# Attention, layer norm and a SiLU feed-forward in one kernel: head triples across chunks, a progressive layer norm, block transposes, one chain for both last projections

## Chip, cores, metric

One core of one Trainium2 chip. The metric is the device time of one execution in microseconds (us). A run more than 1.5% above the fastest of its kernel counts as slow and is left out. A ratio is the mean time of one kernel's fast runs over the mean of the other kernel's fast runs of the same rounds, so it is not quite the ratio of the medians that are quoted beside it.

## The reference

```python
# x: (1, 2048, 640) bf16; H = 32 heads of Dh = 20; one shared K and V head; F = 1728
xn = (x - mean(x)) / sqrt(var(x) + 1e-5)
q  = (xn @ wq).reshape(1, S, 32, 20).transpose(0, 2, 1, 3)
k, v = xn @ wk, xn @ wv                       # (1, 2048, 20) each
p  = softmax(einsum("bhqd,bkd->bhqk", q, k) * 20 ** -0.5)
o  = einsum("bhqk,bkd->bhqd", p, v)
out = x + o.transpose(0, 2, 1, 3).reshape(1, S, 640) @ wo + silu(xn @ w1) @ w2
```

There are 32 x 2048 x 2048 exponentials, and all of them go through ScalarE.

## The kernel before

Queries are handled in 4 chunks of 512 columns. Within a chunk the heads go in groups of three (the last group has two). For each group the 16 key tiles are walked: one *step* is up to three score matmuls (K = 32, side by side in different rows of the array), one exponential over their PSUM banks (128x1536), and up to three value matmuls (side by side in different columns) that add into U. Everything else on TensorE (queries of the next chunk, FFN, output projection) is *side work*. It goes through one PSUM bank, in pieces between the steps, in program order.

```python
for qc in range(QC):                      # 4 chunks
    for g in range(NG):                   # 11 groups: 10 of three heads, 1 of two
        for kt in range(KT):              # 16 key tiles
            steps.append((qc, g, kt))     # 704 steps
# ... (cut)
for t in range(T):
    # ... (cut)
    if t + NSB < T:
        emit_S(t + NSB, 1)                # scores, two steps ahead
    emit_PV(t)
    # ... (cut)
    if kt == KT - 1:
        schedule_U_pipeline(t, misc)      # copy U, 4 f32 TensorE transposes, normalise
    misc_step(BUDGET)                     # BUDGET = 1.1: two 512-wide side matmuls

def misc_step(budget):
    spent = 0.0
    while spent < budget:
        # ... (cut: take the next job)
        job = cur_job[0]
        last = job_emit_mm(job)           # the last matmul also queues VectorE's eviction
        spent += job.weight
        if last:
            cur_job[0] = None             # ... and the next job starts in the same step
```

Before the loop come the layer norm of all 16 row tiles (square root on ScalarE), their TensorE transposes, all of K and V and the first chunk's queries. After it come the transposes of the last chunk's output and its projection.

The softmax here doesn't subtract the row's maximum and nothing guards it: scores larger than these inputs give would overflow.

Of the kernel before, what the change touches and what calls it, by code (L numbers as in the profile page):

```python
# [7 lines left out]
BF16 = mybir.dt.bfloat16  # L8
# [4 lines left out]
P = 128  # L13
D = 640
H = 32
DH = 20
DC = 5
HSLOT = 32
GH = 3
HT = 8  # L20
NE = 4
NHS = 4
BANK = 512
XB = 7
UB = 6
QW = 512
QTP = QW // P
NSB = 2
HWID = 512
HPH = HWID // QW  # L30


class _Prog:

    def __init__(self):
        self.lists = {k: [] for k in ("pe", "act", "dve", "pool", "sp")}
        self.last_wait = {k: {} for k in self.lists}
        self.cnt = defaultdict(int)

    def emit(self, eng, fn):  # L40
        self.lists[eng].append(fn)

    def wait(self, eng, sem, val):
        if val <= 0:
            return
        key = id(sem)
        if self.last_wait[eng].get(key, 0) >= val:
            return
        self.last_wait[eng][key] = val
        self.lists[eng].append(lambda e, s=sem, v=val: e.wait_ge(s, v))  # L50

    def inc(self, sem):
        self.cnt[id(sem)] += 1
        return self.cnt[id(sem)]

    def emit_inc(self, eng, fn, sem):
        val = self.inc(sem)
        self.lists[eng].append(lambda e, fn=fn, s=sem: fn(e).then_inc(s, 1))
        return val


class _Job:
    def __init__(self, name, bank, mms, consumer, cons_eng, cons_sem, pre_waits=(),
                 weight=1.0, after=None, cons_waits=()):
        self.name = name
        self.bank = bank
        self.mms = list(mms)
        self.consumer = consumer
        self.cons_eng = cons_eng
        self.cons_sem = cons_sem  # L70
        self.pre_waits = list(pre_waits)
        self.cons_waits = list(cons_waits)
        self.weight = weight
        self.after = after
        self.idx = 0
        self.min_iter = -1
        self.use_no = None
        self.ready_val = None
        self.cons_val = None


def build(nc, A_x, A_wq, A_wk, A_wv, A_wo, B_x, B_w1, B_w2, out, stack):
    S = A_x.shape[1]
    F = B_w1.shape[1]
    assert A_x.shape[2] == D and S % HWID == 0
    NT = S // P
    QC = S // QW
    KT = S // P
    NHB = S // HWID
    FC = (F + P - 1) // P  # L90
    FLAST = F - (FC - 1) * P
    NG = (H + GH - 1) // GH
    groups = [list(range(g * GH, min(H, (g + 1) * GH))) for g in range(NG)]
    attn_scale = 1.0 / math.sqrt(DH)
    EPS = 1e-5

    pr = _Prog()
    W = pr.wait
    E_ = pr.emit
    EI = pr.emit_inc  # L100

    def sem(name):
        return stack.enter_context(nc.semaphore(name))

    sb_count = [0]

    def sb(shape, dt):
        sb_count[0] += 1
        return stack.enter_context(nc.sbuf_tensor(f"sbt{sb_count[0]}", shape, dt))

    ps = stack.enter_context(nc.psum_tensor("psall", [P, 8 * BANK], F32))

    def bk(b, lo=0, hi=BANK, rows=P):
        return ps[0:rows, b * BANK + lo: b * BANK + hi]

# [3 lines left out]
    XR = 6  # L119
    x_ring = sb([P, XR, D], BF16)  # L120
    xres = sb([P, QTP, D], BF16)
    xn_ring = sb([P, 4, D], BF16)
    xnT = sb([P, DC, S], BF16)
    stats6 = sb([P, NT, 2, 6], F32)
    mv = sb([P, NT, 2], F32)
    rstd = sb([P, NT], F32)
    stdv = sb([P, NT], F32)
    nbias = sb([P, NT], F32)
    ident_b = sb([P, P], BF16)
    ident_f = sb([P, P], F32)  # L130

    wq_st = sb([P, DC, D], BF16)
    wq_pad = sb([P, DC, HT * P], BF16)
    wk_rep = sb([P, DC, P], BF16)
    wv_aug = sb([P, DC, HSLOT], BF16)
    wo_sb = sb([P, DC, D], BF16)
    w1_sb = sb([P, DC, F], BF16)
    w2_sb = sb([P, FC, D], BF16)

    kT_rep = sb([P, S], BF16)  # L140
    v_aug = sb([P, KT, HSLOT], BF16)
    qT = sb([P, HT, 2, QW], BF16)

    Ebuf = sb([P, NE, GH * QW], BF16)
    U_sb = sb([P, 2, QW], F32)
    rL = sb([P, QTP, GH], F32)
    o_norm = sb([P, 2, QTP, D], BF16)
    oT = sb([P, 2, DC, QW], BF16)
    h_half = sb([P, NHS, HWID], BF16)
    t_buf = sb([P, NHS, HWID], BF16)  # L150
    hT = sb([P, 2, FC, HWID], BF16)
    yx = sb([P, QTP, D], F32)
    out_stage = sb([P, 3, D], BF16)

    s_xload = [sem(f"xload{i}") for i in range(XR)]
    s_xres = [sem(f"xres{i}") for i in range(QTP)]
    s_outdma = [sem(f"outdma{i}") for i in range(3)]
    s_wsmall = sem("wsmall")
    s_w1 = sem("w1")
    s_w2 = sem("w2")  # L160
    s_wo = sem("wo")
    s_stats = sem("stats")
    s_std = sem("std")
    s_nb = sem("nb")
    s_xn_a = sem("xna")
    s_xn_d = sem("xnd")
    s_xnT_d = sem("xnTd")
    s_xnT_a = sem("xnTa")
    s_ident = sem("ident")
    s_pmem = sem("pmem")  # L170
    s_prepq = sem("prepq")
    s_wkv = sem("wkv")
    s_prepkv = sem("prepkv")
    s_kT = sem("kT")
    s_v = sem("v")
    s_q = sem("q")
    s_S = sem("S")
    s_E = sem("E")
    s_PV = sem("PV")
    s_Ufree = sem("Ufree")  # L180
    s_norm = sem("norm")
    s_hh = sem("hh")
    s_th = sem("th")
    s_hc = sem("hc")
    s_y = sem("y")
    s_oT = sem("oT")
    s_outp = sem("outp")
    s_ldve = sem("ldve")
    s_lpool = sem("lpool")
    bank_ready = [sem(f"bkr{b}") for b in range(8)]  # L190
    bank_uses = [0] * 8
    bank_last_free = [None] * 8

    def job_start(job):
        b = job.bank
        job.use_no = bank_uses[b]
        bank_uses[b] += 1
        for (s_, v_) in job.pre_waits:
            W("pe", s_, v_)
        if bank_last_free[b] is not None:  # L200
            W("pe", bank_last_free[b][0], bank_last_free[b][1])

    def job_emit_mm(job):
        k = job.idx
        last = (k == len(job.mms) - 1)
        f = job.mms[k]
        b = job.bank
        if last:
            job.ready_val = EI("pe", lambda pe, f=f, b=b: f(pe, b), bank_ready[b])
        else:  # L210
            E_("pe", lambda pe, f=f, b=b: f(pe, b))
        job.idx += 1
        if last:
            ce = job.cons_eng
            for (s_, v_) in job.cons_waits:
                W(ce, s_, v_)
            W(ce, bank_ready[b], job.ready_val)
            run = job.consumer(b)
            job.cons_val = EI(ce, lambda e, run=run: run(e), job.cons_sem)
            bank_last_free[b] = (job.cons_sem, job.cons_val)  # L220
            if job.after is not None:
                job.after(job)
        return last

    def run_job_now(job):
        job_start(job)
        while not job_emit_mm(job):
            pass

    xv = A_x[0].rearrange("(n p) d -> p n d", p=P)  # L230
    outv = out[0].rearrange("(n p) d -> p n d", p=P)
    xn_val = {}

    def sp_load_x_tile(n):
        slot = n % XR
        if n >= XR:
            for (s_, v_) in xn_val[n - XR]:
                W("sp", s_, v_)
        pr.inc(s_xload[slot])
        E_("sp", lambda e, n=n, slot=slot: e.dma_start(x_ring[:, slot, :], xv[:, n, :]).then_inc(s_xload[slot], 16))  # L240

    stats_val = {}

    std_val = {}
    nb_val = {}

    def dve_ln_stats(n):
        slot = n % XR
        half = D // 2
        W("dve", s_xload[slot], 16 * (n // XR + 1))  # L250
        EI("dve", lambda v, n=n, slot=slot: v.bn_stats(stats6[:, n, 0, :], x_ring[:, slot, 0:half]), s_ldve)
        c2 = EI("dve", lambda v, n=n, slot=slot: v.bn_stats(stats6[:, n, 1, :], x_ring[:, slot, half:D]), s_ldve)
        W("dve", s_ldve, c2)
        c3 = EI("dve", lambda v, n=n: v.bn_aggr(mv[:, n, :], stats6[:, n, :, :]), s_ldve)
        W("dve", s_ldve, c3)
        stats_val[n] = EI("dve", lambda v, n=n: v.tensor_scalar_add(stdv[:, n:n + 1], mv[:, n, 1:2], EPS), s_stats)

    def act_ln_sqrt(n):
        W("act", s_stats, stats_val[n])
        std_val[n] = EI("act", lambda a, n=n: a.activation(stdv[:, n:n + 1], stdv[:, n:n + 1], AF.Sqrt), s_std)  # L260

    def dve_ln_rstd(n):
        W("dve", s_std, std_val[n])
        c4 = EI("dve", lambda v, n=n: v.reciprocal(rstd[:, n:n + 1], stdv[:, n:n + 1]), s_ldve)
        W("dve", s_ldve, c4)
        nb_val[n] = EI("dve", lambda v, n=n: v.scalar_tensor_tensor(
            out=nbias[:, n:n + 1], in0=mv[:, n, 0:1], scalar=-1.0, in1=rstd[:, n:n + 1],
# [748 lines left out]
```

## Time and profile before

The median of the first three runs was 1109.26 us (1108.57 to 1115.64).

| stage of the trace | us |
|---|---|
| start to first exponential | 56.6 |
| first group of 16 steps | 23.5 |
| the other 43 groups, to the end of the last exponential | 1014.2 |
| tail | 15.3 |

The page of the kernel before, its busy table and three rows of its 40 slices. A digit is the busy share of a slice in tenths, 9 meaning 90% or more; the clock row is the granted TensorE clock (the share of full speed that its throttle lets it run at) in tenths.

```profile
span 1109.5 us, 13550 instructions
...
PE 917.3 (83%) x5519; PEld 255.4 (23%) x5580; DVE 220.5 (20%) x600; ACT 1000.1 (90%) x819; POOL 24.3 (2%) x61
...
PE   3778789888888878888898878888898878888888
...
ACT  5599999999989998999989998999998988989994
...
PEclk9899979765579998988559997989557988886556
```

ScalarE (ACT) is the busiest, yet never full for long. The clock row shows that TensorE (PE) ran many stretches at half speed.

Groups of instructions of the kernel before: line, engine, operation, shapes, count, then busy us, mean ns of one, and the idle time just before them with what ended it. L663 is the exponential, L688 the TensorE transpose of U.

```profile
L663 ACT ACTIVATE sbt<-psall 128x1536 bf16<-128x1536 f32 (+1 forms) x704 | 947.1, 1453 | 70.0 <-PE psall L590 65.1
...
L688 PE MATMUL psall<-sbt 96*128 96x96 f32 (+1 forms) x176 | 39.8, 318 | 33.1 <-DVE sbt L681 13.4
```

The exponentials wait 65.1 us for score matmuls (L590). The timeline of ScalarE (start us, length us, what, how many) gives the price of one exponential:

```profile
332.56 6.82 ACT L663 ACTIVATE sbt<-psall 128x1536 bf16<-128x1536 f32 x5 [0.28 <-PE psall L590]
339.92 2.79 ACT L663 ACTIVATE sbt<-psall 128x1536 bf16<-128x1536 f32 x2 [0.54 <-PE psall L590]
```

Five in a row take 6.82 us. Less one latency of 1.46, that is 1.34 us for each further one. (The Trainium skill, "ScalarE: Activation LUTs", *What ACT_TABLE_LOAD costs*, gives 186 ns + 0.833 ns per column and an overlap of about 93 ns between neighbours, so an estimate from that page is 1.466 us alone and 1.373 in a row; the trace has 1.45 for one alone, at 343.25 us, and 1.34 in a row.) So 16 three-head steps cost ScalarE at least 21.3 to 21.4 us, and each tanh of the FFN 0.52 us more (from 100.91 to 101.43 in the trace).

Three groups of 16 steps in the windows view (stretch, length, busy us and instruction count of PE, weight loads, VectorE, ScalarE and GpSimd, the granted clock, DMA share, GB/s): one without side work, one with query and FFN first-layer work, one with FFN second-layer work.

```profile
268.78:291.12 22.34, 19.31 (x102) 4.05 (x99) 1.52 (x6) 21.70 (x17) 0.00 (x0) 0.50 0.00 1
336.57:362.26 25.69, 20.73 (x130) 5.62 (x131) 6.17 (x13) 23.04 (x19) 0.00 (x0) 0.93 0.00 1
746.46:768.08 21.62, 18.43 (x138) 5.82 (x136) 3.19 (x9) 21.56 (x18) 0.00 (x0) 1.00 0.03 8
```

The first is at half clock and nearly at ScalarE's limit. The second is at nearly full clock and is over 3 us above it (21.3 plus 2 tanh of 0.52 is 22.4 us at least, measured 25.69). Why, the view of waits tells (who waits, for whom, us in total, times, longest):

```profile
ACT sbt L663 <- PE psall L590: 65.1, 106, 1.8
...
PEld psall L738 <- DVE sbt L745: 36.3, 44, 1.2
...
PE psall L738 <- DVE sbt L745: 23.9, 41, 0.9
```

L738 is the FFN first-layer matmul, L745 VectorE's eviction of its bank. The next job wants the same bank while VectorE still reads it, and the scores of the next step stand behind that job in TensorE's order. Over all lines of this view, weight loads wait 170 us and matmuls 116 us for VectorE (sums of mine; the two overlap).

### The profile page before, as it was taken

Reading aid. Unit: us, or ns where it says so; the run is one execution under the profiler, and the core shown is the slowest. Engines: PE = TensorE matmul, PEld = TensorE weight load, DVE = VectorE, ACT = ScalarE, POOL = GpSimd, SP = SyncE. Lnnn points to the kernel's source line nnn. Section 1 sums busy time; section 2 is a strip of 40 time slices with the busy share of each in tenths; the row PEclk is TensorE's granted clock in tenths of the full one; section 3 lists DMA queues with packets and bytes.
Section 4 is the critical chain, followed back from the end, with each engine's and each line's share of the span. In section 5 each row is a group of like instructions: output and inputs, shape, how many; then the busy total and the mean of one; then the engine's idle time right before and its main releaser. Section 6 shows DMA issues by size and latency. Waiting matters only on the chain.

```text
span 1109.5 us, 13550 instructions
## 1 busy us (share of the span) xinstructions
PE 917.3 (83%) x5519; PEld 255.4 (23%) x5580; DVE 220.5 (20%) x600; ACT 1000.1 (90%) x819; POOL 24.3 (2%) x61
## 2 busy tenths in 40 slices
PE   3778789888888878888898878888898878888888
PEld 2322212221122222222112222222112222222113
DVE  6312321110012332110012232111002331100012
ACT  5599999999989998999989998999998988989994
POOL 8000000000000000000000000000000000000000
PEclk9899979765579998988559997989557988886556
DMA  7200000000000000000000000000000000000000
GB/s 245 96 1 1 1 1 6 13 7 1 1 1 1 1 1 18 12 13 7 1 1 1 1 1 7 18 13 12 1 1 1 1 1 24 1 1 1 1 1 24
DMA packets 9311, 14.86 MB, mean 13 GB/s; under 512 B 1552, under 2 KB 8336, under 8 KB 9248
## 3 DMA queue, kind: packets, MB, share of 16 engines
q1 hardware_dynamic: 7632, 8.69, 2.5%
q0 software_dynamic: 1616, 5.30, 1.4%
q8 instruction: 44, 0.72, 0.3%
q14 instruction: 19, 0.16, 0.0%
HBM read 11.36 MB, written 2.62 MB: 13 GB/s over the span
## 4 chain that ended last, share of the span: by engine, by line
PE 45%; ACT 28%; issue 15%; DVE 9%; POOL 1%; DMA 1%; another core or an unknown queue 1%; DVEq 0%; ACTq 0%; POOLq 0%
ACT sbt L663 25%; PE psall L590 15%; PE psall L622 13%; PE psall L443 4%; PE psall L785 4%; PE psall L738 3%; PE psall L688 3%; PE psall L836 2%; ACT sbt L756 2%; DVE sbt L745 2%; DVE sbt L681 1%; DVE sbt L451 1%; DVE sbt L706 1%; DVE sbt L844 1%
## 5 line engine op out<-in xcount | busy, mean ns | idle before, releaser
L663 ACT ACTIVATE sbt<-psall 128x1536 bf16<-128x1536 f32 (+1 forms) x704 | 947.1, 1453 | 70.0 <-PE psall L590 65.1
L590 PE MATMUL psall<-sbt 32*128 32x512 bf16 x2048 | 339.5, 472 | 67.6 <-ACT sbt L663 46.9
L622 PE MATMUL psall<-sbt 128*32 128x512 bf16 x2048 | 343.2, 477 | 0.4 <-ACT sbt L663 0.2
L590 PEld LDWEIGHTS psall<-sbt 32*128 32x128 bf16 x2048 | 70.7, 94 | 316.2 <-ACT sbt L663 224.2
L622 PEld LDWEIGHTS psall<-sbt 128*32 128x32 bf16 x2048 | 72.2, 96 | 222.3 <-issue 216.8
L738 PE MATMUL psall<-sbt 128*128 128x512 bf16 (+1 forms) x259 | 88.7, 404 | 28.8 <-DVE sbt L745 23.9
L785 PE MATMUL psall<-sbt 128*128 128x128 bf16 (+3 forms) x432 | 100.2, 328 | 10.5 <-DVE sbt L792 5.5
L681 DVE COPY sbt<-psall 96x512 f32<-96x512 f32 (+1 forms) x44 | 30.2, 687 | 319.9 <-PE psall L622 319.9
L688 PE MATMUL psall<-sbt 96*128 96x96 f32 (+1 forms) x176 | 39.8, 318 | 33.1 <-DVE sbt L681 13.4
L745 DVE TENSOR_SCALAR sbt<-psall 128x512 bf16<-128x512 f32 (+1 forms) x56 | 38.6, 690 | 137.3 <-PE psall L738 135.0
L443 PE MATMUL psall<-sbt 128*128 128x512 bf16 x148 | 48.8, 418 | 10.6 <-DVE sbt L451 7.1
L792 DVE TENSOR_TENSOR sbt<-psall,sbt 128x512 f32<-128x512 f32 (+1 forms) x32 | 15.7, 491 | 177.5 <-PE psall L785 177.5
L785 PEld LDWEIGHTS psall<-sbt 128*128 128x128 bf16 x448 | 29.8, 102 | 67.6 <-issue 46.5
L836 PE MATMUL psall<-sbt 128*128 128x128 bf16 (+1 forms) x150 | 33.8, 334 | 7.2 <-DVE sbt L844 3.2
L766 DVE SCALAR_TENSOR_TENSOR sbt<-sbt 128x512 bf16<-128x512 bf16 (+1 forms) x56 | 38.0, 680 | 0.0
L756 ACT ACTIVATE sbt<-sbt 128x512 bf16<-128x512 bf16 (+1 forms) x56 | 37.4, 667 | 0.0
L688 PEld LDWEIGHTS psall<-sbt 96*128 96x128 f32 (+1 forms) x176 | 22.0, 167 | 61.6 <-DVE sbt L681 33.1
L738 PEld LDWEIGHTS psall<-sbt 128*128 128x128 bf16 (+1 forms) x280 | 18.5, 98 | 74.0 <-DVE sbt L745 36.3
L451 DVE CAST sbt<-psall 128x512 bf16<-128x512 f32 x24 | 16.6, 690 | 75.8 <-PE psall L443 73.0
L844 DVE TENSOR_TENSOR sbt<-psall,sbt 128x512 bf16<-128x512 f32 (+1 forms) x32 | 15.3, 490 | 56.6 <-PE psall L836 50.8
L706 DVE TENSOR_TENSOR sbt<-psall,sbt 128x60 bf16<-128x60 f32 (+1 forms) x176 | 26.1, 210 | 1.5
L699 DVE RECIPROCAL sbt<-psall 128x12 f32<-128x12 f32 (+1 forms) x44 | 10.1, 230 | 77.8 <-PE psall L688 77.8
(47 smaller groups left out, 176.8 us busy)
## 6 DMA issues: line engine op xcount, KB each, us to landing
sbt<-in_A_x_dram SPq DMA_DIRECT2D x32, 160.0 KB, 2.5
out_dram<-sbt SPq DMA_DIRECT2D x16, 160.0 KB, 1.8
sbt<-in_B_w_dram POOLq DMA_DIRECT2D x5, 432.0 KB, 5.4
sbt<-in_B_w_dram POOLq DMA_DIRECT2D x13, 160.0 KB, 6.6
sbt<-in_A_wq_dram SPq DMA_DIRECT2D x5, 160.0 KB, 3.7
sbt<-in_A_wo_dram POOLq DMA_DIRECT2D x5, 160.0 KB, 6.9
sbt<-in_A_wv_dram POOLq DMA_DIRECT2D x5, 5.0 KB, 3.2
sbt<-in_A_wk_dram POOLq DMA_DIRECT2D x5, 5.0 KB, 2.3
```

What stands on the lines that cost most here:

```text
L443: return pe.matmul(bk(b, 0, QW), wq_pad[:, c, ht * P:(ht + 1) * P], xnT[:, c, qc * QW:(qc + 1) * QW], start=(c == 0), stop=(c == DC - 1))
L590: return pe.matmul(s_out_ap(t, i), kT_rep[s_ * HSLOT:(s_ + 1) * HSLOT, kt * P:(kt + 1) * P], qT[s_ * HSLOT:(s_ + 1) * HSLOT, ht, par, :], ...
L622: return pe.matmul(ps[i * HSLOT:(i + 1) * HSLOT, UB * BANK:UB * BANK + QW], v_aug[:, kt, :], Ebuf[:, e, e_col(i):e_col(i) + QW], start=(kt ...
L663: a.activation(Ebuf[:, t % NE, 0:width], ps[:, base:base + width], AF.Exp, scale=attn_scale).then_inc(s_E, 1)
L681: Ufree_val[n] = EI("dve", lambda v, upar=upar, rows=rows: v.tensor_copy(U_sb[0:rows, upar, :], ps[0:rows, UB * BANK:UB * BANK + QW]), s_U ...
L688: return pe.transpose(ps[:, b * BANK + qt * RS: b * BANK + qt * RS + rows], U_sb[0:rows, upar, qt * P:(qt + 1) * P], ident_f[0:rows, 0:rows])
L738: return pe.matmul(bk(b, 0, HWID, rows=rows), w1_sb[:, c, fk * P:fk * P + rows], xnT[:, c, hb * HWID:(hb + 1) * HWID], start=(c == 0), sto ...
L745: return lambda v: v.tensor_scalar_mul(h_half[0:rows, slot, :], bk(b, 0, HWID, rows=rows), 0.5)
L756: a.activation(t_buf[0:rows, slot, :], h_half[0:rows, slot, :], AF.Tanh).then_inc(s_th, 1)
L766: E_("dve", lambda v: v.scalar_tensor_tensor(out=hT[0:rows, hb % 2, fk, :], in0=t_buf[0:rows, slot, :], scalar=1.0, in1=h_half[0:rows, slo ...
L785: return pe.matmul(bk(b, 0, N_), hT[0:rows, hpar, fk, hcol:hcol + P], w2_sb[0:rows, fk, e0:e1], start=(fk == 0), stop=(fk == FC - 1))
L836: return pe.matmul(bk(b, 0, N_), oT[:, opar, c, i * P:(i + 1) * P], wo_sb[:, c, e0:e1], start=(c == 0), stop=(c == DC - 1))
```

## The change

The intent: start exponentials as soon as four row tiles are normalised; let triples run across the chunks, so that 128 (chunk, head) units make 43 groups instead of 44 and only the last is short; take the transposes of U off TensorE; make FFN second layer and output projection one accumulation; pace the side work by what is left of it.

The diff replaces nearly the whole file. Its core, with cuts marked by `...`:

```diff
-for qc in range(QC):
-    for g in range(NG):
-        for kt in range(KT):
-            steps.append((qc, g, kt))
+units = [(u // H, u % H) for u in range(QC * H)]
+groups = [units[i:i + GH] for i in range(0, len(units), GH)]
+steps = [(g, kt) for g in range(len(groups)) for kt in range(KT)]
 ...
-...   (cut: U copied to SBUF, 4 f32 TensorE transposes, reciprocal, 4 products, later 5 bf16 transposes per row tile)
+def emit_norm(t):
+    ...
+    op("dve", lambda v: v.transpose(U_sb[0:rows, p, :], bk(UB, r1=rows)), r=["U"], w=[("Us", p)])
+    ...   # reciprocal and product on VectorE
+        op("dve", lambda v, ...: v.transpose(
+            oT[s0 * SLOT:s1 * SLOT, par, ht, :], O_sb[s0 * SLOT:s1 * SLOT, p, :]), ...)
 ...
-...   (cut: ffn2, 14 matmuls of 512 and of 128 columns, into yx; outp, 5 of each, added to yx)
+def y_job(qc, i, e):      # 14 + 8 matmuls of 320 columns in one accumulation, two halves
+    return Job(("y", qc, i, e), y_mms(qc, i, e, True, range(HT), XB), 140, lambda: y_out(qc, i, e, XB, "x"))
 ...
-BUDGET = 1.1
+def misc(t):
+    spent = 0
+    per = min(qc for qc in range(QC) if t < period_end[qc] or qc == QC - 1)
+    left = sum((len(j.mms) - j.idx) * j.cost + GAP for j in queue + cur if j is not None and j.period <= per)
+    budget = min(640, max(200, left / max(1, period_end[per] - t - 6)))
+    while spent < budget and (queue or cur[0] is not None):
+        cost, end = advance(t)
+        if cost is None or end:       # a job's end ends the step's side work
+            return
+        spent += cost
 ...
-...   (cut: layer norm of all 16 tiles, K, V and queries before the loop)
+...   (cut: 4 tiles before the loop, with TensorE transposes; tiles 4..15 by VectorE, GpSimd (power) and
+...    DMA transposes; K and V blocks 1..3 as jobs that the scores and value matmuls call for)
```

The last chunk is different: its FFN chain and the first 6 of its 8 output tiles are summed ahead (into `ya`) in the last 44 steps, and only two tiles are left for the tail.

## The prediction

> **What bounds it now.** ScalarE: busy 1000.1 of 1109.5 us, 947.1 of it in 704 exponentials (busy table, groups by line). Three stages in the timeline: a prologue (layer norm of all 16 row tiles, K, V, first queries) until the first exponential at 56.6 us; the loop, to 1094; a tail of 15 us. Five back-to-back 128x1536 exponentials take 6.82 us, so one costs 1.34 (6.82 less one latency of 1.46, over four); a tanh between two costs 0.52. So 640 x 1.34 + 64 x about 1.0 + 56 x 0.52 = 950 us of ScalarE in 1038 us of loop: some 85 us are lost to TensorE.
>
> How (windows, timeline): its clock is granted at 1.0 or 0.5 ("TensorE: Matmul & The Clock Gate", part 1, has these two states, in 3.4 us windows; the trace agrees: 0.50 at 1060:1090, 1.00 at 100:150). Stretches without side work run at 0.5 and need 1.395 us a step; two side matmuls per step (queries, FFN first layer) make it 1.55 to 1.63 at a clock near 1; FFN second layer 1.33 at clock 1.0, 1.54 at 0.79. Two-head steps (64) take 1.19 us for two thirds of the work.
>
> **The change.**
> 1. Exponentials start after 4 tiles, not 16. VectorE spends about 1.75 us a tile (0.48+0.48+0.21+0.15+0.45); I put the first exponential at 17 us. Tiles 4 to 15 come through VectorE and DMA transposes during the first group: about 7 us per four tiles against 5.4 of exponentials, plus latencies: some 8 us of stalls. Net gain about 31 us. "VectorE: DVE Perf Modes" (the three transpose paths) gives 1.3 us for a 128x128 DMA transpose; no trace here shows one yet.
> 2. Triples across chunks: 672 three-head and 16 two-head steps instead of 640 and 64. 64 x 1.19 becomes 32 x 1.39 + 16 x 1.19: about 13 us.
> 3. U is transposed in 32x32 blocks on VectorE. TensorE loses 176 f32 transposes (39.8 us busy plus 22.0 of weight loads) and 80 bf16 ones (11.0); VectorE (20% busy) gains little. Group boundaries, now 0.9 us above 16 x 1.34, get a bit cheaper.
> 4. Both projections in one chain of 22 matmuls of 320 columns: the padded output matrix adds about 9% columns; evictions halve.
> 5. Side work is spread evenly, about 320 ns a step, one job end per step, so evictions hide. Idle stretches fill, heavy ones thin. But at clock 0.5 a step then needs 0.54+0.54+0.64 us, over 1.34: dips still cost.
> 6. Tail: two K chunks of output projection, about 10 us.
>
> **Sum.** 47 us to the end of group one + 656 x 1.40 (918) + 18 for the short group + 22 of tanh not hidden + 10 = 1015 us; range 980 to 1052. Faster by over 2%: 0.96; within 2%: 0.03; slower: 0.01.
>
> **What would show it.** First exponential at 15 to 20 us; group one 27 to 34 us long; 688 exponentials; mean step 1.37 to 1.43 without tanh; ScalarE over 93% busy; mean clock 0.8 to 0.9; last exponential to end 8 to 12 us.
>
> **What would make it wrong.** The clock staying at 0.5 under thin even load (steps of 1.5, about 1080 us); slow DMA transposes starving K (plus 10 to 25 us); VectorE releasing U late, behind other work; or the clock staying at 1.0 (steps of 1.35, 982 us).

## The result

| | median us | range | runs |
|---|---|---|---|
| before | 1112.45 | 1108.57 to 1121.72 | 4 |
| after | 1040.93 | 1038.53 to 1041.71 | 4 |

The ratio is 0.931 (95% interval 0.925 to 0.938). A later repeat on another chip gave 1040.76 us and 0.927.

| stage of the trace | before | after | gain | predicted after |
|---|---|---|---|---|
| start to first exponential | 56.6 | 15.8 | 40.8 | 17 |
| first group | 23.5 | 32.0 | -8.6 | 30 |
| all other groups | 1014.2 | 982.1 | 32.1 | 958 |
| tail | 15.3 | 10.0 | 5.3 | 10 |
| sum | 1109.5 | 1039.9 | 69.6 | 1015 |

The page of the changed kernel, the same rows as above:

```profile
span 1039.9 us, 12209 instructions
...
PE 887.4 (85%) x5393; PEld 235.8 (23%) x5438; DVE 242.8 (23%) x460; ACT 966.2 (93%) x756; POOL 23.1 (2%) x39
...
PE   8797788779889888789988888879989988888998
...
ACT  4889999898989999999999999999999999999874
...
PEclk8989999885689999975579999985557999555995
```

ScalarE is at 93%, but the clock row still has four dips. Groups of the changed kernel: L417 is the exponential, L434 VectorE's transpose of U out of PSUM.

```profile
L417 ACT ACTIVATE sb<-psall 128x1536 bf16<-128x1536 f32 (+1 forms) x688 | 935.9, 1607 | 30.2 <-PE psall L408 28.0
...
L434 DVE STREAM_TRANSPOSE sb<-psall 128x512 f32<-128x512 f32 (+1 forms) x43 | 30.8, 717 | 297.1 <-PE psall L425 297.1
```

Waits of the changed kernel (L480 is the FFN first-layer matmul, L485 its eviction, L505 the FFN part of the last chain, L519 its eviction):

```profile
ACT sb L417 <- PE psall L408: 28.0, 53, 2.9
PEld psall L480 <- DVE sb L485: 26.8, 52, 2.7
...
PE psall L480 <- DVE sb L485: 10.6, 8, 2.4
...
PEld psall L505 <- DVE sb L519: 5.6, 10, 1.2
```

The exponentials' wait for scores fell from 65.1 to 28.0 us, and so did side work's wait for VectorE: over all lines, 67 us for weight loads and 30 us for matmuls, from 170 and 116. Windows of the changed kernel: two groups with the last chain, two with FFN first-layer work, three with none, and the last two groups with the pre-sum of the last chunk.

```profile
338.16:380.75 42.59, 35.40 (x259) 10.33 (x257) 6.41 (x12) 42.59 (x33) 0.00 (x0) 1.00 0.01 5
706.23:757.69 51.46, 50.04 (x221) 10.04 (x223) 13.11 (x21) 48.03 (x39) 0.00 (x0) 0.50 0.00 1
890.44:954.92 64.48, 55.65 (x291) 10.26 (x288) 7.91 (x14) 64.48 (x50) 0.00 (x0) 0.50 0.00 1
979.10:1029.90 50.80, 47.19 (x271) 15.66 (x268) 7.76 (x15) 39.42 (x33) 0.00 (x0) 0.81 0.00 1
```

Two groups with the last chain take 42.59 us, 1.331 us a step: ScalarE is never idle, at full clock. Three without side work take 64.48 (1.343 a step) at half clock: ScalarE is never idle either. But the two in 706:758 take 51.46 us for the same 32 exponential steps plus 6 tanh (45.7 us of ScalarE), at half clock, with TensorE 97% busy. Much of the missing time is in such stretches, and their side work is *thin*: 28 side matmuls in 32 steps.

The start, in ScalarE's timeline of the changed kernel (L304 copies a block of K):

```profile
15.75 4.13 ACT L417 ACTIVATE sb<-psall 128x1536 bf16<-128x1536 f32 x3 [0.55 <-PE psall L408]
23.60 0.60 ACT L304 ACTIVATE sb<-psall 128x512 bf16<-128x512 f32 x1 [3.71 <-PE psall L297]
24.09 5.47 ACT L417 ACTIVATE sb<-psall 128x1536 bf16<-128x1536 f32 x4
31.49 0.60 ACT L304 ACTIVATE sb<-psall 128x512 bf16<-128x512 f32 x1 [1.93 <-PE psall L297]
...
40.64 0.60 ACT L304 ACTIVATE sb<-psall 128x512 bf16<-128x512 f32 x1 [3.18 <-PE psall L297]
```

The first group stalls three times for a K block, 3.71 + 1.93 + 3.18 = 8.8 us (8 were predicted).

### The profile page after: what moved, and what is told of

The parts are those of the page before. It is cut to its first block, busy times and chain, and to the rows that moved or that the text cites. A ratio compares the mean times of both kernels' runs of the same rounds, so it can differ in the third digit from the quotient of the medians.

```text
span 1039.9 us, 12209 instructions
## 1 busy us (share of the span) xinstructions
PE 887.4 (85%) x5393; PEld 235.8 (23%) x5438; DVE 242.8 (23%) x460; ACT 966.2 (93%) x756; POOL 23.1 (2%) x39
## 4 chain that ended last, share of the span: by engine, by line
ACT 66%; PE 27%; DVE 5%; issue 1%; DMA 1%; SPq 0%; DVEq 0%
ACT sb L417 63%; PE psall L408 8%; PE psall L425 8%; PE psall L480 5%; PE psall L505 2%; ACT sb L487 2%; DVE sb L449 1%; PE psall L326 1%; DVE sb L434 1%; PE psall L510 1%; DVE sb L485 1%; DVE sb L438 1%; DMA sb<-in_A_wq_dram 1%; PE psall L297 1%; DVE sb L437 0%
## 5 line engine op out<-in xcount | busy, mean ns | idle before, releaser
L417 ACT ACTIVATE sb<-psall 128x1536 bf16<-128x1536 f32 (+1 forms) x688 | 935.9, 1607 | 30.2 <-PE psall L408 28.0
L408 PE MATMUL psall<-sb 32*128 32x512 bf16 x2048 | 321.0, 459 | 112.7 <-ACT sb L417 92.4
L425 PE MATMUL psall<-sb 128*32 128x512 bf16 x2048 | 325.0, 465 | 1.7 <-DVE sb L317 1.0
L408 PEld LDWEIGHTS psall<-sb 32*128 32x128 bf16 x2048 | 68.7, 93 | 378.1 <-ACT sb L417 304.6
L480 PE MATMUL psall<-sb 128*128 128x512 bf16 (+1 forms) x253 | 109.9, 474 | 13.5 <-DVE sb L485 10.6
L425 PEld LDWEIGHTS psall<-sb 128*32 128x32 bf16 x2048 | 70.2, 95 | 208.3 <-issue 193.1
L505 PE MATMUL psall<-sb 128*128 128x320 bf16 x448 | 95.5, 312 | 6.5 <-DVE sb L536 3.5
L434 DVE STREAM_TRANSPOSE sb<-psall 128x512 f32<-128x512 f32 (+1 forms) x43 | 30.8, 717 | 297.1 <-PE psall L425 297.1
L485 DVE CAST sb<-psall 128x512 bf16<-128x512 f32 (+1 forms) x56 | 38.4, 686 | 175.5 <-PE psall L480 150.3
L326 PE MATMUL psall<-sb 128*128 128x512 bf16 (+1 forms) x160 | 51.9, 396 | 10.0 <-DVE sb L334 7.7
L510 PE MATMUL psall<-sb 128*128 128x320 bf16 x256 | 57.5, 318 | 2.0 <-DVE sb L449 2.0
L519 DVE SCALAR_TENSOR_TENSOR sb<-psall,sb 128x320 bf16<-128x320 f32 x32 | 15.4, 484 | 154.3 <-PE psall L510 153.9
L505 PEld LDWEIGHTS psall<-sb 128*128 128x128 bf16 x448 | 32.9, 98 | 56.5 <-issue 36.6
L449 DVE STREAM_TRANSPOSE sb<-sb 96x512 bf16<-96x512 bf16 (+2 forms) x64 | 45.2, 706 | 2.1
L334 DVE CAST sb<-psall 128x512 bf16<-128x512 f32 x31 | 21.3, 686 | 88.9 <-PE psall L326 82.6
L480 PEld LDWEIGHTS psall<-sb 128*128 128x128 bf16 (+1 forms) x280 | 22.6, 101 | 80.4 <-issue 52.2
L510 PEld LDWEIGHTS psall<-sb 128*128 128x128 bf16 x256 | 19.6, 101 | 30.5 <-issue 21.4
L438 DVE TENSOR_TENSOR sb<-sb 128x320 bf16<-128x320 f32 (+1 forms) x43 | 21.1, 492 | 1.5
L326 PEld LDWEIGHTS psall<-sb 128*128 128x128 bf16 x175 | 11.5, 98 | 32.4 <-issue 21.1
```

The lines of the kernel that those rows point to most:

```text
L326: "pe", lambda pe: pe.matmul(bk(bank, c0, c1), wq[:, c, t, :], xnT[:, c, qc * QW + c0:qc * QW + c1], start=(c == 0), stop=(c == DC - 1)),
L408: op("pe", lambda pe, i=i, s=s, ht=ht, qc=qc: pe.matmul(bk(ring(t) + i), kT[s * SLOT:(s + 1) * SLOT, kt * P:(kt + 1) * P], qT[s * SLOT:(s ...
L417: op("act", lambda a: a.activation(E[:, t % NE, 0:n * QW], ps[:, b:b + n * QW], AF.Exp, scale=scale), r=[("B", ring(t) + i) for i in range ...
L425: op("pe", lambda pe, i=i, s=s: pe.matmul(bk(UB, r0=s * SLOT, r1=(s + 1) * SLOT), v_aug[:, kt, :], E[:, t % NE, i * QW:(i + 1) * QW], star ...
L434: op("dve", lambda v: v.transpose(U_sb[0:rows, p, :], bk(UB, r1=rows)), r=["U"], w=[("Us", p)])
L449: op("dve", lambda v, s0=s0, s1=s1, par=par, ht=ht: v.transpose(oT[s0 * SLOT:s1 * SLOT, par, ht, :], O_sb[s0 * SLOT:s1 * SLOT, p, :]), r=[ ...
```

## Theory and rival

The total is 25 us over the prediction, and the stage table puts 24 of them into the groups after the first.

**Theory A.** The pacing rule, whose floor is 200 ns, falls to one 512-wide side matmul per step when the queue runs low. So little side work leaves the clock at 0.5, and at 0.5 a step of scores (0.54), values (0.55) and one side matmul (0.54, each from its start to the next one's in 706:758) is longer than 1.34: TensorE becomes the limit. Either less side work (none) or more (two matmuls) would be faster.

**Theory B.** These stretches are slow for what they hold: the tanh makes a round trip from VectorE to ScalarE and back, and the bank has to be emptied. The clock is a bystander, and TensorE at 97% busy cannot take more.

Each part of the change was also undone or put back by itself. All kernels gave correct results. The experiments ran on four chips, so differences are taken across chips; the eight runs of the changed kernel went from 1036.5 to 1044.4, and a few us are not told apart.

## Experiments

Each kernel starts from the changed one (median 1040.8 us in its repeat) unless said otherwise.

### e4_floor_420: two side matmuls at least

```diff
-        budget = min(640, max(200, left / max(1, period_end[per] - t - 6)))
+        budget = min(640, max(420, left / max(1, period_end[per] - t - 6)))
```

> The changed kernel with the least side work of a step raised from 200 to 420 ns of matmul (two 512-wide matmuls a step instead of one where the schedule runs thin). Theory A (the 26 us over the prediction come from stretches with one side matmul a step, in which the clock stays at 0.5 and TensorE itself sets a step of 1.6 us): the FFN first-layer stretches run at a clock of 0.9 or more with 1.50 to 1.55 us a step tanh included, the idle stretches after them at 1.34, total 1012 to 1028 us. Theory B (these stretches are slow because of the tanh round trip through VectorE and the shared PSUM bank, whatever the clock): denser side work does not help or hurts, 1038 to 1060 us.

Measured: 1021.88 us (1018.67 to 1022.68), 19 us less, inside theory A's range and outside B's. The windows of this kernel, two groups (27 and 28, counting from 0) dense with FFN first-layer work, and two (30 and 31) with no side work:

```profile
650.03:698.33 48.30, 36.89 (x241) 9.72 (x246) 18.99 (x31) 48.30 (x44) 0.00 (x0) 1.00 0.00 1
723.34:765.93 42.59, 36.90 (x195) 6.83 (x192) 5.74 (x10) 42.59 (x34) 0.00 (x0) 0.50 0.00 1
```

The dense groups run at a clock of 1.00 with ScalarE never idle, tanh and all; the same 14 jobs are over sooner, and the idle groups after them cost 1.331 us a step at half clock. The first try had a floor of 430, which is just over the 426 that the code books for two such matmuls and so allowed three a step. Jobs then followed each other so fast that the buffer of three half-activations was written while its last reader was still queued.

### e5_zero_matmuls: twice the work, for nothing

```diff
+                op("pe", lambda pe: pe.matmul(bk(XB, r1=rows), zero[:, 0:rows],
+                                              xnT[:, c, qc * QW:(qc + 1) * QW], start=False, stop=(c == DC - 1)),
+                   r=["zero"] + [("xnT", n) for n in range(qc * TPQ, (qc + 1) * TPQ)], w=[("B", XB)])
```

(after each FFN first-layer matmul; the sum gets zeros added)

> The changed kernel with pure waste added: after each of the 280 FFN first-layer matmuls one more of the same size with a weight of zeros into the same sum (same result, 280 more matmuls[...]). Theory A (thin side work leaves the clock at 0.5): the added work lifts the clock to 1.0 in these stretches, a step falls from 1.6 to about 1.5, and the kernel gets faster[...]: 1015 to 1032 us. Theory B: TensorE is the limit there as it stands, so the work adds 0.2 to 0.4 us to each of those steps: 1070 to 1120 us.

Measured: 1034.06 us (1028.54 to 1034.37). This is 7 us faster with 280 more matmuls, and just above the range given for A. The window of two groups that answers to 706:758 of the changed kernel:

```profile
703.38:749.16 45.78, 39.14 (x252) 9.88 (x253) 13.03 (x21) 45.78 (x40) 0.00 (x0) 1.00 0.00 1
```

The same two groups fall from 51.46 to 45.78 us: the clock is 1.00, TensorE is *less* busy (39.14 us instead of 50.04) with more to do, and ScalarE is never idle. This settles that the clock, and not the tanh or the evictions, made these stretches slow, for tanh, evictions and schedule are untouched. (The profiled run is the fastest of the four, 1028.54.) The total gains less because the waste also falls on stretches that were dense already: the second and third groups with FFN work go from 23.89 and 24.23 us to 24.62 and 25.27.

The groups 26 to 31 (96 steps, the third chunk) hold the same 14 FFN first-layer jobs in all these kernels, though those with the raised floor have done some of the last-chain work before; ScalarE's own work in them is 96 x 1.33 + 14 x 0.52 = 135 us:

| kernel | groups 26 to 31, us |
|---|---|
| after | 146.4 |
| e5, zero matmuls | 139.8 |
| e4, floor 420 | 138.4 |
| e11, below | 135.8 |

### e1_full_prologue: step 1 undone

```diff
     for n in range(2 * TPQ + 3, KT + 2):
-        at((1, 2, 2, 4, 4, 5, 5)[n - 2 * TPQ - 3], lambda n=n: ln_next(n))
+        ln_next(n)
+    for b in range(1, KT // 4):      # all of K and V, too
+        ...
+    special.clear()
```

> The changed kernel with the layer norm of all 16 tiles, all of K and all of V ahead of the first exponential; the rest untouched. If the early start is worth what the prediction gave it (31 us), this takes about 1072 us. Rival: most of the shorter start comes from a layer norm that is simply quicker (1.27 us a tile on VectorE in the trace of after, done at 26 us), and the overlap itself is worth little: the first exponential comes at about 36 us, the first group then takes 22 us without stalls and ends near 59 instead of 47.8, and the total is about 1052 us.

Measured: 1051.62 us (1050.66 to 1052.49): 11 us, the rival's number. ScalarE's timeline of this kernel:

```profile
35.58 5.72 ACT L417 ACTIVATE sb<-psall 128x1536 bf16<-128x1536 f32 x4 [0.54 <-PE psall L408]
41.76 20.25 ACT L417 ACTIVATE sb<-psall 128x1536 bf16<-128x1536 f32 x15 [0.46 <-PE psall L408]
```

The first exponential comes at 35.6 us, the first group takes 22.2 us and ends at 57.7. In the kernel before it ended at 80.0, in the changed one at 47.8. So of the 32 us gained up to there, 22 belong to a prologue that is quicker in itself, and 10 to starting early. What makes it quicker was not tested part by part; the traces show no ScalarE square root between the tiles, one query tile instead of eight up front, and no 7.6 us wait for the load of a row tile, which the chain of waits of the kernel before has from 22.4 us on. The prediction had the sum right (31) and gave all of it to the early start.

### e2_chunk_triples: step 2 undone

```diff
-    groups = [units[i:i + GH] for i in range(0, len(units), GH)]
+    groups = [units[c + i:c + min(i + GH, H)] for c in range(0, QC * H, H) for i in range(0, H, GH)]
```

(and the function that gives a head's first step to match)

> The changed kernel with its head triples cut at the chunk's end, as in the kernel before: 44 groups, 640 three-head and 64 two-head steps. The prediction's estimate is 13 us: about 1054 us. Rival: the short steps are only as dear as ScalarE makes them (1.07 us at best, 48 of them more, 32 long ones of 1.33 fewer, so 9 us) or they let the side work through, so that almost nothing changes: 1041 to 1050 us.

Measured: 1052.49 us (1049.79 to 1058.73), 12 us. The estimate (13) holds in size; the two explanations, 13 from the kernel before and 9 from ScalarE alone, are too near each other for this run to part them.

### e6_pe_transposes: step 3, TensorE's part put back as dead work

```diff
+        j = Job(("ut", g), [back(qt) for qt in range(TPQ)], 100, lambda: op("dve", ...))   # 4 f32 96x96 transposes
+        j.period = 0
+        queue.insert(0, j)
```

> The changed kernel with the TensorE part of the old normalisation put back as dead work beside the new one: per group four f32 96x96 transposes of U into the side bank, and a small VectorE read of them, as a job at the head of the queue (results unchanged). If the removed transposes were on the path, as the prediction's step 3 lets one think (62 us of TensorE), they cost 20 to 50 us: 1061 to 1090. If they were mostly hidden behind ScalarE, the cost is under 12 us: 1036 to 1053, and it can even help where the clock sits at 0.5.

Measured: 1057.11 us (1056.43 to 1065.88): 16 us, between the two ranges. In groups without other side work it costs 1.0 us per group (22.5 instead of 21.5), which is also the level of the kernel before (22.34, above). 43 x 1.0 would be 43 us; most of it is hidden where ScalarE is the limit at full clock (groups 12, 13, 23 and 24 stay at 21.3). It is a putting-back of load, not the old code: VectorE's share of the old scheme and the 80 bf16 transposes are not in it.

### e3_two_chains: step 4 undone for three chunks

```diff
-    def y_job(qc, i, e):
-        return Job(("y", qc, i, e), y_mms(qc, i, e, True, range(HT), XB), 140, lambda: y_out(qc, i, e, XB, "x"))
+    # yf_job: 14 FFN matmuls, evicted into the f32 tile ya;  yo_job: 8 output matmuls, added to ya
```

> The changed kernel with the FFN's and the attention's last projection as two chains (14 and 8 matmuls, the first added into an f32 tile, the second on top of it) for the first three chunks; 24 more jobs, the same matmuls. If one chain matters through its evictions (prediction, step 4): 6 to 20 us slower, 1047 to 1061. Rival: evictions are hidden by the pacing, within 5 us of 1041.

Measured: 1056.08 us (1053.73 to 1064.82), 15 us, with no more matmuls than before and only 24 more evictions. The trace has the loss in three groups (14, 25 and 26: 28.9, 28.0 and 26.7 us instead of 21.3, 21.3 and 21.8), in which the mean clock fell to 0.56 to 0.58. The sum of waits for VectorE hardly moved (80 us for weight loads instead of 67), but the trace shows where the clock fell. Here it is at 363.1 us (L510 is the output projection, L449 transposes at a group's end, L530 the eviction of the FFN chain):

```profile
362.65 0.45 DVE L530 SCALAR_TENSOR_TENSOR sb<-psall,sb 128x320 f32<-128x320 f32 x1
...
363.16 0.71 PE L510 MATMUL psall<-sb 128*128 128x320 bf16 x2 [2.20 <-DVE sb L530]
```

The new second chain waits 2.20 us for an eviction that stands behind the normalisation of U; at the other fall, 622.6 us, it waits 1.46. The clock then stays at 0.5 for 27.3 and 47.8 us, with TensorE busy for all but 0.06 and 0.69 us of them. No run takes this wait away, so it is read from the trace and not shown by experiment; e9 and e11 below test the same pattern elsewhere.

### e7b_no_stop_200: one rule of step 5 taken away

```diff
-            if cost is None or end:
+            if cost is None:
                 return
```

> The changed kernel without the rule that a step ends its side work at a job's end: the next job's matmuls follow at once in the same step and so wait for VectorE to empty the bank (0.69 us plus the handover) with the next scores behind them. If hiding the eviction matters (prediction, step 5), slower by 8 to 30 us: 1050 to 1070, with waits of the side matmuls for VectorE up from some 45 us in all. Rival: the budget of a thin step is mostly used up by then, so nothing changes, or the denser work even lifts the clock: 1030 to 1046.

Measured: 1091.13 us (1088.11 to 1097.65). The direction is the expected one, but at 50 us the size is far over the range. Waits of this kernel, to be read against those of the changed kernel above:

```profile
ACT sb L417 <- PE psall L408: 60.9, 106, 2.7
...
PEld psall L480 <- DVE sb L485: 42.9, 52, 3.0
...
PEld psall L505 <- DVE sb L519: 24.6, 21, 3.5
...
PE psall L480 <- DVE sb L485: 22.3, 20, 2.7
```

The exponentials' wait is back near the 65.1 of the kernel before, and the mean clock falls from 0.815 to 0.757. Where TensorE stands waiting for a bank it can lose twice, the wait and then steps at half clock: in group 26 a side matmul waits 3.30 us for VectorE, and the group takes 30.8 us at a mean clock of 0.56 instead of 21.8 at 1.00.

### e10_before_stop: the same rule given to the kernel before

```diff
             if last:
                 cur_job[0] = None
+                return
```

> The kernel before, with one rule of the changed one: a step ends its side work at a job's end. If the rule is worth in the kernel before what its removal cost the changed one (50 us), it takes 1060 to 1090 us with all else as it was. Rival: it matters only with the changed kernel's thin pacing; in the kernel before, whose steps always hold two wide matmuls, it gives under 15 us: 1097 to 1125.

Measured: 1074.45 us (1071.93 to 1075.57), against 1119.94 for the kernel before in the same rounds: ratio 0.957 (0.951 to 0.962), about 45 us from one line. The waits for VectorE fall to 82 us for weight loads and 37 us for matmuls (from 170 and 116), the exponentials' wait for scores from 65.1 to 33.1. Of its waits, to be read against those of the kernel before:

```profile
ACT sbt L663 <- PE psall L590: 33.1, 66, 1.5
...
PEld psall L738 <- DVE sbt L745: 6.0, 19, 0.5
...
PE psall L738 <- DVE sbt L745: 1.0, 5, 0.2
```

With e7b, this rule has the largest single effect that any part of the change showed. It also thins the side work at each job's end, and no run parts that from the shorter waits.

### e8_floor_split: towards a better kernel

The floor of e4, and the last chunk's FFN chain moved out of the crowded last 44 steps into the idle groups before them.

```diff
-        return Job(("y", qc, i, e), y_mms(qc, i, e, True, range(NPRE), XB), 140, done, first=...)
+        if ffn:
+            return Job(("yf", qc, i, e), y_mms(qc, i, e, True, (), XB), 140, done)
+        return Job(("y", qc, i, e), y_mms(qc, i, e, False, range(NPRE), XB), 140, add, first=...)
```

> The pacing floor of 420 ns and, besides, the last chunk's FFN chain moved out of the last 44 steps into the idle stretch before them (8 jobs of 14 matmuls; the 6 ready tiles of the attention projection are added on top later). Theory A (what costs is side work at clock 0.5, or so dense that it fills the step; idle stretches are free): the last three groups, which take 25.0, 25.2 and 22.3 us with the floor alone, fall to about 22, 22 and 19, total 1008 to 1017 us. Rival: the stretch only trades places, 1018 to 1028.

Measured: 1012.37 us (1007.41 to 1015.15). The last three groups take 23.0, 23.3 and 17.5 us.

### e9_warm_idle: holding the clock up in idle steps

```diff
-        misc(t)
+        if not misc(t):
+            warm(2, XB)      # two matmuls of zeros into the free side bank
```

> The kernel of the floor and the split chain (1012 us), and in every step that has no side work two dead matmuls of zeros into the free side bank, to hold the clock up. Theory A: idle stretches stay at 1.33 us a step (ScalarE sets them at either clock), and the slow steps at each return of side work (groups of 22.5 to 25 us at a mean clock of 0.6 to 0.8) shrink towards 21.3: mean clock over 0.95, total 994 to 1006 us. Rival: the dead work delays scores and the idle stretches grow: 1012 to 1030 us.

Measured: 1010.35 us (1007.05 to 1013.08): a miss, for neither range holds it. The mean clock did rise to 0.979 and idle groups are at 21.3 us, but idle groups had been almost free before. Nine short drops of the clock were left inside the loop (a tenth falls in the tail), eight of them where a side matmul waits for VectorE, 1.46 to 2.40 us, at the end of a group. One of them in the timeline of this kernel (L438 and L449 belong to the normalisation of U, L334 empties the side bank of a query job, L326 is the next query job):

```profile
286.98 0.25 DVE L437 RECIPROCAL sb<-sb 128x16 f32<-128x16 f32 x1
...
287.27 0.49 DVE L438 TENSOR_TENSOR sb<-sb 128x320 bf16<-128x320 f32 x1
287.79 1.44 DVE L449 STREAM_TRANSPOSE sb<-sb 64x512 bf16<-64x512 bf16 x2
289.17 0.64 DVE L334 CAST sb<-psall 128x512 bf16<-128x512 f32 x1
...
289.87 0.61 PE L326 MATMUL psall<-sb 128*128 128x512 bf16 x2 [2.40 <-DVE sb L334]
...
290.89 1.45 ACT L417 ACTIVATE sb<-psall 128x1536 bf16<-128x1536 f32 x1 [1.53 <-PE psall L408]
```

At a group's end VectorE gets the whole normalisation at once, about 3 us with the transpose out of PSUM. It takes its instructions in order (the Trainium skill, "TensorE: Matmul & The Clock Gate", *Architectural detail*, calls its queue strictly first in, first out; the trace agrees, with 0.64 us of eviction waiting behind 2.2 us of burst). The side matmul waits 2.40 us, the exponential 1.53, and from 290.7 us the clock is at 0.5 for 3.4 us.

### e11_spread_norm: the burst spread over four or five steps

```diff
+        def soon(k, fn):
+            fn() if t == T - 1 else at(t + k, fn)
-        op("dve", lambda v: v.reciprocal(rl, Uv[:, :, DH]), r=[("Us", p)], w=[("rL", p)])
+        soon(1, lambda: op("dve", lambda v: v.reciprocal(rl, Uv[:, :, DH]), r=[("Us", p)], w=[("rL", p)]))
         ...   # the product at soon(2, ...), the bf16 transposes at soon(3, ...) and soon(4, ...)
```

> The kernel of the floor, the split chain and the warm idle steps (1010 us), with the work after U's transpose spread: the reciprocal, the product and the one or two bf16 transposes go to VectorE one per step in the next four or five steps instead of all at once at the group's end. In the trace of the kernel it starts from, nearly every drop of the clock (at 55, 127, 195, 291, 448, 540, 697, 956 us) begins where a side matmul waits 1.5 to 2.7 us for VectorE to empty its bank behind that burst of some 3 us. Theory: without the burst these waits shrink under 1 us, most drops vanish, and some 2 to 3.5 us each come back: 985 to 997 us. Rival: the drops have another cause, or the delayed work only moves the wait: 1003 to 1015 us.

Measured: 987.43 us (986.8 to 988.2, six runs); ratio to the kernel before of the same rounds 0.888 (0.883 to 0.892). Of the page of this kernel:

```profile
span 985.4 us, 12905 instructions
...
PE 848.8 (86%) x5732; PEld 248.6 (25%) x5798; DVE 242.9 (25%) x468; ACT 953.2 (97%) x756; POOL 23.1 (2%) x39
...
PEclk9999999999999999999999999999999999999999
```

Two drops of the clock are left, one in the first group and one in the tail. From 500 to 900 us ScalarE is busy for all 400 (its window, in the columns of the windows above):

```profile
500.00:900.00 400.00, 353.18 (x2435) 106.03 (x2450) 82.47 (x146) 400.00 (x308) 0.00 (x0) 1.00 0.01 4
```

What is left above ScalarE's own work is the start, the stalls of the first group, some 2 us in the last, short group and the tail.

## Why the prediction was right, and where it was off

The prediction (1015 us, 980 to 1052) holds the measured 1040.9, and the direction is the predicted one. Point by point:

- **Bound by ScalarE, 85 us lost to TensorE: right.** With the clock held and the evictions out of the way (e11) the loop runs at ScalarE's rate.
- **Step 1, net gain about 31 us: right in size (32), wrong in its account.** e1 shows 10 to 11 us for the early start; 22 are a quicker prologue. First exponential (17 predicted, 15.8), stalls (8, 8.8), end of the first group (47, 47.8) all held. The DMA transposes were not slow: issued about every 1.3 us, landing in 2.6.
- **Step 2, 13 us: e2 says 12.**
- **Step 3, unsized there beyond TensorE's busy time:** putting its load back costs 16 us, so about a quarter of the 62 us is on the path.
- **Step 4, padding +9% columns, evictions halved: unsized.** Two chains cost 15 us more.
- **Step 5, evenly spread side work of about 320 ns a step: this step failed in part.** The work is not spread evenly: the floor of the rule leaves stretches with one matmul a step and stretches with none. The mean step came to 1.414 us without tanh (956.5 us of 656 steps, less 56 tanh of 0.52), inside the stated 1.37 to 1.43 but over the 1.40 of the sum; the tanh, counted in full, are 29.1 us instead of 22; and the last, short group took 25.6 us instead of 18, because the pre-sum of the last chunk was crowded into the last 44 steps. The terms that were too small: 918 + 22 us measured 956.5, and 18 measured 25.6; that is the 24 us. The prediction listed the cause (the clock staying at 0.5 under thin even load) as a way to be wrong, for the whole kernel; the chip did it in three stretches. By the times of the groups, their eight groups (8, 9, 18 to 20, 29 to 31) cost 20.5 us over ScalarE's own work, of 54 for groups 1 to 41 together, where the prediction's sum left room for 38. e4, which packs this side work denser, gets 19 back in all: 14 in these eight, 3 in the last group. The prediction does not say how its 1.40 follows from steps 3 to 5; that the mean came so near it is in part luck.
- **The same step named "one job end per step, so evictions hide" without a number.** It is the dearest part: 50 us when taken from the changed kernel, about 45 when given to the one before.
- **Step 6, tail about 10 us: 10.0.**

The undone parts add up to 11 + 12 + 16 + 15 + 50 = 104 us against a gain of about 72 in the medians. They are not independent: each of them makes TensorE wait or work longer at some places, and the clock can then turn a wait into more slow steps (as in group 26 of e7b), so that single effects overlap. Left open are what exactly lifts the clock from 0.5 (below), and whether the waits that the trace of e3 shows are all that let it fall there.

## What to carry to other kernels

When one engine sets the pace and TensorE serves it from one in-order stream, look for where TensorE waits inside a step: let side work stop at the end of a job, so that its bank is empty before it is wanted again, and do not hand VectorE a burst just when it must empty a bank. Read the granted clock beside the busy share: a stretch that is 97% busy at half clock may need more work per step, or none. Dead work in steps that are already free buys little (2 us here, inside the spread of the runs); moving real work there bought 10.

## What the Trainium skill lacked or had wrong

- "TensorE: Matmul & The Clock Gate", Part 1: two clock states and 3.4 us windows agree with every trace here. But the page has full clock follow from a busy window of about 3.4 us. Here TensorE was 97% busy by the profile from 706 to 758 us (50.04 of 51.46) and the clock stayed at 0.5, in one piece for 92 us, in the repeat as well; with twice the 128-row matmuls in the same steps it was 1.00. So busy time in the profile is not what decides (the page says this of transposes alone); one 128x128x512 side matmul a step, beside the 32-row and 32-column ones, was too little and two were enough. The rule behind it is not known from these runs.
- The same page does not say that a single wait of 1.46 to 2.40 us of a matmul inside a dense stretch can be followed by a drop to 0.5 for 3.4 to 6.8 us (eight places in e9, all gone in e11, where no such wait after the first group is over 0.39 us). It speaks of idle gaps over about 3.4 us, and of micro-idles that make the clock swing, without their length. Such a wait does not decide alone: waits of 1.29 and 1.37 us in the changed kernel were followed by no drop, and in e10 the clock drops 25 times in the loop though no matmul there waits over 1 us for VectorE.
- "VectorE: DVE Perf Modes", *The three transpose paths*: it gives 311 ns for 128x128 bf16 on VectorE and 1309 ns by DMA. These runs add 0.72 us for 128x512 f32 out of PSUM, 0.71 us for 128x512 bf16 (0.70 for 32 partitions too), and for a 128x640 bf16 DMA transpose a median of 2.6 us to landing, with one issued about every 1.28 us.
- No page that I read gives GpSimd's power of a 128x1 column: 0.55 to 0.70 us here (median 0.68), against 0.20 us for ScalarE's square root in the kernel before.
